# A row-tiled pair for the half-filled rows of unseparated projections, the output weights in two transfers, and a new timetable, in a transformer block

## The chip, the core and the metric

The kernel runs on one core of a Trainium2 chip. The metric is the time of one execution on the device in microseconds; the median of the runs is compared. TensorE (PE, with its weight loads shown as PEld) multiplies, VectorE (DVE), ScalarE (ACT) and GpSimd (POOL) work on elements, and SyncE (SP) issues nearly all DMA transfers.

## The reference

One transformer block in bf16 on 2048 tokens of width 576: layer norm, attention with 32 heads of 18 and a running memory over 4 segments of 512 tokens, residual, layer norm, a feed-forward of width 4608, residual.

```python
h = x + _A_ref(_layernorm(x), wq, wk, wv, wo, beta)
h2 = h + _B_ref(_layernorm(h), w1, b1, w2, b2)
# _A_ref, for each segment s of 4, per head:
p = _softmax(qs @ ks.T * scale + causal_mask)
a_dot = p @ vs
pq = phi(qs)                       # phi(t) = t + 1 where t > 0, else exp(t)
a_mem = (pq @ M) / (pq @ z + 1e-06)
o = g * a_mem + (1.0 - g) * a_dot  # g = sigmoid(beta)
M, z = M + phi(ks).T @ vs, z + phi(ks).sum(over tokens)
# after all segments: o @ wo; _B_ref: gelu(x @ w1 + b1) @ w2 + b2
```

## The kernel before

The work of a segment is cut into stages, and the names below are the tags of its operations. X normalises four tiles of 128 tokens and brings them into transposed form: the first ones by TensorE (`TX`), the others by a store to DRAM (`X1dma`) and a transposing load (`X1flip`). P projects each tile to q, k and v and writes q and k out padded (`qkst`); transposing loads (`A0flip`, `A1flip`, ...) bring them back for the attention. A computes scores (`st`), exponentials (`exp`), causal masks (`mask`), weighted values (`val`) and, from segment 1 on, the read of the memory (`mem`); M adds to the memory. B is the output projection, the residual (`hadd`), the second layer norm and its transposition, C the first feed-forward product with its evictions (`copy`) and the gelu, D the second product and the last residual. Stages of different segments overlap.

The width of 576 is four blocks of 128 rows and one of 64. The weights hold a fifth block, k = 4, in which the first 288 output columns have their last 64 rows in partitions 0 to 63, the other 288 in partitions 64 to 127; the remaining partitions of that block are zero. A projection of one tile (`proj_pair`) has two forms:

- Separated. `fn_a` (P) runs, for each of five blocks, two matmuls with 64 rows each, side by side on the two row halves of TensorE, the upper half for one half of the columns (one PSUM bank), the lower for the other. Then a marker on DVE or POOL (`pass`) separates the halves, and `fn_b` (R) runs four more such pairs with the banks exchanged. That is 10 + 8 matmuls, in nine pairs. Other work stands between P and R.
- Unseparated (`fused`), when the timetable puts R right behind P: ten full matmuls of 128 rows, five for each half of the columns, the zero partitions included.

TensorE thus works in four modes: full, two row tiles of 64, four row tiles of 32 (scores), and four column tiles of 32 (values, and some reads of the memory).

The order of the work is written out by hand as data. `TIMETABLE` gives for each operation a rank and an engine; `Graph.schedule` sorts by rank, runs a cost model in which each operation has planned costs, and picks buffers and PSUM banks. The costs in the `add` calls are planned costs in microseconds: they decide which buffer is taken, not what is issued. Each engine then executes its instructions in that order, and waits in the order's place when something isn't ready. SyncE too issues its transfers in the order of the timetable, `load_w` with one transfer for a whole weight. In the modes' part of `schedule`, a change of mode is planned with 0.1 us.

Of the kernel before, what the change touches and what calls it, by code (L numbers as in the profile page):

```python
# [11 lines left out]
ACT = mybir.ActivationFunctionType  # L12
# [7 lines left out]
FUSED = 1.225  # L20
INF = 1e9
# [322 lines left out]
}  # L344


# [1278 lines left out]
```

## Time and profile before

| | |
|---|---|
| median of 3 runs | 440.25 us (439.9 to 440.84) |
| span of the profiled execution | 439.3 us; the page gives no time of that execution beside it |
| TensorE busy | 431.0 us (98%), 5182 matmuls, granted clock 1.000 |
| DVE, ACT, POOL busy | 288.5, 298.2, 176.5 us |
| DMA | 75.61 MB, 172 GB/s |

In a row of groups stand line, engine, operation, what it writes and reads, shapes and count, then busy time, mean ns of one, and the idle time of the engine before it with what ended it. Matmuls are pipelined, so the duration of one is longer than the time in which the next follows. The chain of waits lists start, length and what in order of time; two matmuls side by side on row tiles count as two.

### The profile page before, as it was taken

What the parts mean: (1) busy time and instruction counts of PE and PEld (TensorE: products, weight loads), DVE (VectorE), ACT (ScalarE), POOL (GpSimd) and SP (SyncE); (2) the same over time, 40 slices, a digit from 0 to 9 for tenths busy, and PEclk for the clock granted to TensorE, in tenths of its full rate; (3) what the DMA queues carried; (4) which work ended last, traced back from release to release, by engine and by line L of the source; (5) the groups of instructions that cost most, each with busy time, mean ns of one, the idle gap of its engine ahead of it and who ended that gap; (6) DMA issues with size and microseconds to landing.
All of it is one profiled execution on the core that took longest, in us unless ns stands there. A gap on an engine that the chain in (4) does not pass through costs nothing.

```text
span 439.3 us, 12412 instructions
## 1 busy us (share of the span) xinstructions
PE 431.0 (98%) x5182; PEld 279.0 (64%) x5182; DVE 288.5 (66%) x641; ACT 298.2 (68%) x325; POOL 176.5 (40%) x328
## 2 busy tenths in 40 slices
PE   8998999999999999999999999999999999999997
PEld 5665677776677676664445766654457785446886
DVE  5898889988997987975698897766776211000002
ACT  5997988999888897788898976657864003465000
POOL 6676866445867644571631462320203001020001
PEclk9999999999999999999999999999999999999999
DMA  7699999989899758973671859506405752450011
GB/s 229 214 209 230 347 262 273 234 274 229 236 235 340 196 157 231 229 157 101 155 185 26 243 152 213 107 18 213 140 25 143 233 131 81 151 175 1 1 58 51
DMA packets 80280, 75.61 MB, mean 172 GB/s; under 512 B 57952, under 2 KB 67424, under 8 KB 80224
## 3 DMA queue, kind: packets, MB, share of 16 engines
q1 hardware_dynamic: 80080, 74.74, 63.9%
q8 instruction: 40, 0.66, 0.7%
q14 instruction: 16, 0.13, 0.1%
q10 hardware_dynamic: 144, 0.09, 0.1%
HBM read 42.30 MB, written 18.87 MB: 139 GB/s over the span
## 4 chain that ended last, share of the span: by engine, by line
PE 89%; DMA 4%; DVE 3%; SPq 1%; POOL 1%; ACT 1%; issue 1%; DVEq 0%; POOLq 0%
PE bank L1453 33%; PE bank L1364 24%; PE bank L859 9%; PE bank L1401 8%; PE bank L1227 4%; PE bank L885 3%; PE bank L1252 3%; DMA xreg<-xnd 2%; DMA x<-in_A_x_dram 2%; PE bank L1201 1%; PE bank L1098 1%; PE bank L1067 1%; SPq L663 1%; SPq L670 1%; PE bank L1198 1%
## 5 line engine op out<-in xcount | busy, mean ns | idle before, releaser
L1016 ACT ACTIVATE pt<-bank 128x1024 bf16<-128x1024 f32 x160 | 155.5, 1021 | 36.7 <-PE bank L1227 26.5
L1453 PEld LDWEIGHTS <-hT 128*128 128x128 bf16 x1188 | 111.3, 98 | 33.4 <-issue 6.6
L1364 PE MATMUL bank<-xreg,w1g 64*128 64x512 bf16 x972 | 107.7, 377 | 0.0
L1364 PEld LDWEIGHTS <-w1g 64*128 64x128 bf16 x972 | 46.2, 94 | 57.2 <-issue 3.0
L1453 PE MATMUL bank<-w,hT 128*128 128x288 bf16 (+2 forms) x594 | 77.8, 283 | 0.0
L1453 PE MATMUL bank<-w_lo,hT 128*128 128x288 bf16 (+2 forms) x594 | 77.6, 283 | 0.0
L1466 DVE TENSOR_TENSOR ot<-bank,hc 128x288 bf16<-128x288 f32 (+2 forms) x33 | 14.1, 444 | 85.1 <-PE bank L1453 79.6
L1241 POOL TENSOR_SCALAR_AFFINE_SELECT pt<-pt 128x512 bf16<-128x512 bf16 x57 | 38.0, 680 | 45.4 <-ACT pt L1016 45.1
L1369 ACT ACTIVATE hT<-bank,b_col 128x512 bf16<-128x512 f32 x36 | 22.1, 690 | 46.4 <-PE bank L1364 46.3
L1439 POOL TENSOR_TENSOR hc<-hc,b_bc 128x576 f32<-128x576 f32 x11 | 14.5, 1333 | 83.6 <-DMA hc<-hd 83.6
L1379 DVE TENSOR_SCALAR hT<-bank,b_col 128x512 bf16<-128x512 f32 x45 | 32.6, 742 | 19.4 <-PE bank L1364 17.3
L1401 PE MATMUL bank<-xreg,w1g 64*128 64x256 bf16 x648 | 38.4, 270 | 0.0
L1401 PEld LDWEIGHTS <-w1g 64*128 64x128 bf16 x648 | 30.5, 94 | 6.6 <-issue 3.2
L1384 ACT ACTIVATE hT<-hT 128x8192 bf16<-128x8192 bf16 (+2 forms) x6 | 31.8, 5320 | 0.1
L859 PE MATMUL bank<-hT,xreg 64*128 64x288 bf16 x414 | 27.7, 283 | 1.7 <-DMA xreg<-xnd 1.7
L885 PE MATMUL bank<-hT,xreg 128*128 128x288 bf16 x210 | 28.4, 287 | 0.3 <-ACT pt L1016 0.2
L1412 DVE TENSOR_TENSOR hT<-bank,b_col 128x512 bf16<-128x512 f32 x33 | 21.4, 681 | 6.3 <-PE bank L1401 5.9
L1377 ACT ACTIVATE hT<-bank,b_col 128x512 bf16<-128x512 f32 x27 | 17.8, 686 | 11.4 <-PE bank L1364 11.0
L859 PEld LDWEIGHTS <-xreg 64*128 64x128 bf16 x414 | 19.6, 94 | 8.3 <-DMA xreg<-xnd 1.9
L1227 PE MATMUL bank<-qk 32*128 32x512 bf16 (+3 forms) x384 | 24.2, 301 | 0.2 <-DVE hT L1379 0.2
L885 PEld LDWEIGHTS <-xreg 128*128 128x128 bf16 x210 | 19.7, 98 | 6.4 <-issue 1.0
L773 POOL TENSOR_TENSOR ln<-ln,mhalf 128x1 f32<-128x1 f32 x32 | 19.5, 610 | 2.7
(122 smaller groups left out, 566.4 us busy)
## 6 DMA issues: line engine op xcount, KB each, us to landing
w1g<-in_B_w_dram SPq DMA_DIRECT2D x41, 576.0 KB, 4.9
qkd<-qk_pad SPq DMA_DIRECT2D x15, 512.0 KB, 4.7
hd<-h SPq DMA_DIRECT2D x16, 288.0 KB, 4.6
hc<-hd SPq DMA_DIRECT2D x16, 288.0 KB, 4.0
w_lo<-in_B_w_dram SPq DMA_DIRECT2D x3, 864.0 KB, 7.2
w<-in_B_w_dram SPq DMA_DIRECT2D x3, 864.0 KB, 8.4
xb<-in_A_x_dram SPq DMA_DIRECT2D x16, 144.0 KB, 4.7
x2d<-xn SPq DMA_DIRECT2D x14, 160.0 KB, 2.8
```

Source lines behind the costliest of these rows:

```text
L859: return nc.tensor.matmul(out=half(hf), lhsT=xTb.t[r, k, ts], rhs=wt[r, hf, k, :], start=start, stop=stop, skip_group_check=True)
L885: nc.tensor.matmul(out=half(hf), lhsT=xTb.t[:, k, ts], rhs=wt[:, hf, k, :], start=(k == 0), stop=(k == KT - 1))
L1016: ops.append(add(prio, {"act": 1.04}, lambda e, j=j: nc.scalar.activation(out=pt.t[:, 2 * j:2 * j + 2, :], in_=st[j].t[:], func=ACT.Exp, s ...
L1227: nc.tensor.matmul(out=st[i // 2].t[:, i % 2, off:off + n_], lhsT=qk[rows, 1, kt * P:(kt + 1) * P], rhs=qk[rows, 0, kt * P:L], start=True, ...
L1241: nc.gpsimd.affine_select(out=blk, in_=blk, pattern=[[0, 4], [1, P]], compare_op=ALU.is_ge, fill=0.0, base=0, channel_multiplier=-1)
L1364: nc.tensor.matmul(out=cc[w].t[:], lhsT=w1.t[rows, k, q, :], rhs=x2T[s].t[rows, k, :], start=(k == 0), stop=(k == ND - 1))
L1369: ready_f[f + w] = [add(pf - 12, {"act": 0.68}, lambda e, f=f, w=w, cc=cc: nc.scalar.activation(out=hT[:, :, f + w, :], in_=cc[w].t[:].rea ...
L1379: nc.vector.tensor_scalar(out=dst, in0=src, scalar1=b, scalar2=None, op0=ALU.add)
L1384: ge = add(2.9, {"act": 0.42 * (f1 - f0) + 0.2}, lambda e, f0=f0, f1=f1: nc.scalar.activation(out=hT[:, :, f0:f1, :], in_=hT[:, :, f0:f1, ...
L1401: nc.tensor.matmul(out=cc[w].t[:, q * 2 * P:(q + 1) * 2 * P], lhsT=w1.t[rows, k, q, :], rhs=x2T[s].t[rows, k, ts], start=(k == 0), stop=(k ...
L1412: nc.vector.tensor_tensor(out=dst, in0=src, in1=b.unsqueeze(2).to_broadcast([P, 2, 2 * P]), op=ALU.add)
L1453: nc.tensor.matmul(out=c.t[:, 0:c1 - c0], lhsT=hT[:, tl // 2, f, (tl % 2) * P:(tl % 2 + 1) * P], rhs=w2_c[ch][:, f - ch * WCH, c0:c1], sta ...
```

## The change

An unseparated projection may now take a third form: the four full blocks as full matmuls, and the fifth block as one pair of matmuls with 64 rows, on the two row halves side by side. The pair stands first (`form == "first"`) or last (`"last"`). `schedule` takes it where its cost model finds it cheaper, which is where the neighbour on the pair's side is row-tiled by 64 already. It has eight full matmuls and a pair in place of ten full ones.

The weights of the output projection are loaded in two transfers of one half of the columns each, which may be issued from the time when the first tile is transposed, in place of one transfer behind the last projection of segment 0. Some planned costs change (the first normalisations, one exponential, the gates, and the size of the broadcast of beta). All ranks of the timetable are new, and some operations change engines.

```diff
+TAILED = 1.103
...
 TIMETABLE = {
...
-    "B01tail": "g 330",
+    "B01tail": "d 326",
...
-    "C00dma": "s 261 292 319 395 399 420 421 461 466",
+    "C00dma": "s 242 315 373 374 388 415 424 438 484",
...
-    "P01copy": "a 105 114 109 92 94 143",
+    "P01copy": "d104 d117 a133 a74 a86 a143",
...
-    "X1flip": "s 198",
+    "X1flip": "s 220",
...
-    "X2dma": "s 136 258 310 266 444 400",
+    "X2dma": "s 149 347 285 190 408 401",
...
+    "wodma": "s 100 218",
...
+        for n, op in enumerate(on_pe):
+            op.next_mode = next((o.mode for o in on_pe[n + 1:] if o.mode), "full")
...
             if op.fused:
                 c = 0.0 if op.mate is not None else FUSED
-            kind = op.mode if e == "pe" else op.table
+                if op.mate is None:
+                    was, then = table.get("pe"), op.next_mode
+                    s = SWITCH["pe"]
+                    plain = FUSED + s * (was != "full") + s * (then != "full")
+                    first = TAILED + s + s * (was != "rows64") + s * (then != "full")
+                    last = TAILED + s + s * (was != "full") + s * (then != "rows64")
+                    if min(first, last) < plain - 1e-9:
+                        op.form = "first" if first <= last else "last"
+                        c = TAILED + s + s * (was != ("rows64" if op.form == "first" else "full"))
+                        table["pe"] = kind = "full" if op.form == "first" else "rows64"
...
-                return add(prio, {"dve": 0.55}, apply, [sa, sb, *after, *extra], None, [dst_buf, ma, mb, xsrc], name="apart")
+                return add(prio, {"dve": 0.70}, apply, [sa, sb, *after, *extra], None, [dst_buf, ma, mb, xsrc], name="apart")
...
+                n = KT if b.form is None else KT - 1
+                if b.form == "first":
+                    for w in range(2):
+                        rows(w, w, KT - 1, True, False)
                 for hf in range(2):
-                    for k in range(KT):
-                        nc.tensor.matmul(out=half(hf), lhsT=xTb.t[:, k, ts], rhs=wt[:, hf, k, :], start=(k == 0), stop=(k == KT - 1))
+                    for k in range(n):
+                        nc.tensor.matmul(out=half(hf), lhsT=xTb.t[:, k, ts], rhs=wt[:, hf, k, :], start=(k == 0 and b.form != "first"),
+                                         stop=(k == n - 1 and b.form != "last"), skip_group_check=True)
+                if b.form == "last":
+                    for w in range(2):
+                        rows(w, w, KT - 1, False, True)
...
-        bl = load(2, lambda: beta_bc[:], lambda: A_beta.partition_broadcast(P), 8e3, [xn_ok[0, 0]])
+        bl = load(2, lambda: beta_bc[:], lambda: A_beta.partition_broadcast(P), 250e3, [xn_ok[0, 0]])
...
-        w_ok["o"] = load_w(4, "o", 3, begin)
+        gr.tag = "wo"
+        w_ok["o"] = [load(4, lambda h=h: wts["o"][:, h, :, :].rearrange("p k d -> p (k d)"),
+                          lambda h=h: A_w[3 * P:4 * P, h * KT * HALF:(h + 1) * KT * HALF], 350e3, [xn_ok[0, 0]]) for h in range(2)]
+        gr.tag = ""
```

More of the change, by code (lines that the diff above doesn't have):

```diff
@@ L396, in __init__ @@
         self.alt, self.mate, self.fused, self.fence, self.mode = None, None, False, None, table
+        self.form, self.next_mode = None, None
 OVER = {"act": 0.1, "dve": 0.08, "pool": 0.035}
@@ L461, in schedule @@
             c = op.cost[e]
+            kind = op.mode if e == "pe" else op.table
             if op.fused:
                 c = 0.0 if op.mate is not None else FUSED
-            kind = op.mode if e == "pe" else op.table
+                if op.mate is None:
[8 more added lines that the diff above has]
+                        table["pe"] = kind = "full" if op.form == "first" else "rows64"
             if kind is not None and kind != table.get(e):
@@ L826, in stage_X @@
                 pl = prio + 0.1 * tl if s == 0 else X_PRIO + 0.3 * s + 0.05 * tl
-                ap = layernorm(pl, lambda xb=xb, tl=tl: xb.t[:, tl % 2, :], [ld] + ([xs_pre[0][1], x0b] if s == 0 else []), xb, xn, 0.50, [], tl if (s, tl) in CENTRED else None,
+                ap = layernorm(pl, lambda xb=xb, tl=tl: xb.t[:, tl % 2, :], [ld] + ([xs_pre[0][1], x0b] if s == 0 else []), xb, xn, 0.56, [], tl if (s, tl) in CENTRED else None,
                                ([ld], [ld] if tl else [x0b]) if s == 0 else None, (s, tl // 2) in PE_X)
@@ L1186, in stage_A @@
                 pg = prio + 0.001 * (5 * (g // 2) + 3 * (g % 2))
-                a = add(pg + 0.02, {"act": 0.62}, lambda e, g=g, eb=eb: nc.scalar.activation(out=eb.t[:], in_=qks[g].t[:, 0, :], func=ACT.Exp),
+                a = add(pg + 0.02, {"act": 0.64}, lambda e, g=g, eb=eb: nc.scalar.activation(out=eb.t[:], in_=qks[g].t[:, 0, :], func=ACT.Exp),
                         [qk_ok[g]], eb, [qks[g]], table="exp", name="eg")
@@ L1520, in gmz_fn @@
             nc.gpsimd.tensor_copy(out=gmz[32 * i:32 * i + 32, :, 0:Dh], in_=src.to_broadcast([32, G, Dh]))
-        gates.append(add(2.5, {"dve": 1.7}, gate_fn, [ge], name="gates"))
+        gates.append(add(2.5, {"dve": 0.73}, gate_fn, [ge], name="gates"))
         later.append(gates[0])
         mz_gates = [add(3.55, {"pool": 0.31}, lambda e, i=i: gmz_fn(i), [gates[0]], name="gmz") for i in range(4)]
-        w_ok["o"] = load_w(4, "o", 3, begin)
+        gr.tag = "wo"
+        w_ok["o"] = [load(4, lambda h=h: wts["o"][:, h, :, :].rearrange("p k d -> p (k d)"),
+                          lambda h=h: A_w[3 * P:4 * P, h * KT * HALF:(h + 1) * KT * HALF], 350e3, [xn_ok[0, 0]]) for h in range(2)]
+        gr.tag = ""
         b1_in = Buf(ot_s)
```

625 rows, old and new, of the table TIMETABLE are left out of this document.

## Prediction

> **What bounds the kernel now.** I read the page's head and its slices first, then the busy time by stretches, the chain that ended last, and the list of waits.
>
> ```profile
> span 439.3 us, 12412 instructions
> ...
> PE 431.0 (98%) x5182; PEld 279.0 (64%) x5182; DVE 288.5 (66%) x641; ACT 298.2 (68%) x325; POOL 176.5 (40%) x328
> ...
> PE   8998999999999999999999999999999999999997
> ...
> DVE  5898889988997987975698897766776211000002
> ACT  5997988999888897788898976657864003465000
> ...
> PEclk9999999999999999999999999999999999999999
> DMA  7699999989899758973671859506405752450011
> ```
>
> TensorE is busy for 98% of the span at full clock. DVE, ACT and the DMA queue are near full too, but only in the first half; from slice 5 on they change the time only if they stop TensorE. The busy time by stretches (PE, PEld, DVE, ACT, POOL; clock; DMA share; GB/s) says where TensorE does stop:
>
> ```profile
> 0.00:20.00 20.00, 18.01 (x150) 12.10 (x151) 14.31 (x40) 14.88 (x28) 12.49 (x37) 1.00 0.71 233
> 20.00:40.00 20.00, 16.97 (x324) 12.08 (x322) 19.02 (x48) 18.54 (x23) 15.29 (x33) 1.00 1.00 181
> 40.00:60.00 20.00, 19.65 (x348) 14.09 (x350) 16.88 (x42) 16.72 (x22) 14.89 (x40) 1.00 1.05 322
> 60.00:436.60 376.60, 376.39 (x4367) 240.76 (x4361) 238.04 (x512) 248.03 (x255) 133.86 (x220) 1.00 0.61 161
> ```
>
> After 60 us it idles for 0.2 of 376.6 us; from 20 to 60 us for 3.4, while DVE works 19.0 of 20 us and the DMA share is 1.00. So a change can save time in two ways: fewer columns and mode changes on TensorE, anywhere, or less idle time between 20 and 60 us. The chain shows the longest idle piece, and the list of waits prices it:
>
> ```profile
> 3.85 0.43 SPq L663
> ...
> 26.32 0.91 SPq L663
> 27.33 1.27 SPq L670
> 28.64 1.51 SPq L670
> 30.20 0.59 SPq L663
> 30.90 9.12 DMA xreg<-xnd
> 40.07 2.99 PE bank L859 x46
> ```
> ```profile
> PE bank L859 <- DMA xreg<-xnd: 1.7, 1, 1.7
> ```
>
> SyncE stores two normalised tiles of segment 1 (26.32 is the second store; 3.85 is a plain load, for comparison), issues two transposing loads for the first attention stage, then the whole output weight (30.20), then the transposing load of segment 1's second half (30.90). That one lands at 40.02, and TensorE, which had run dry 1.7 us before, starts on it at 40.07. Everything that TensorE does before 40.07 is thus worth nothing by itself: only an earlier landing is.
>
> **The change on TensorE.** Counted in the two programs: 36 separated and 24 unseparated projections become 34 and 26, and 23 of these 26 take the new form. In slots of 288 columns, where a row-tiled pair is one slot, a separated projection has 9, an unseparated one 10, the new form 9: 564 become 543, 21 fewer. Changes of tiling mode between neighbouring instructions rise from 193 to 215, because the timetable alternates more often; 22 more. Both prices stand in the chain around 166 us:
>
> ```profile
> 164.47 2.21 PE bank L1453 x18
> 166.68 1.20 PE bank L1252 x32
> 167.88 0.33 PE bank L1227 x8
> 168.21 2.31 PE bank L1453 x18
> ```
>
> The first 18 full matmuls follow a full one, the last 18 follow a row-tiled one: 2.21/18 = 0.123 us is a slot, and 2.31 - 2.21 = 0.10 us a mode change. So 21 x 0.123 = 2.58 us go and 22 x 0.10 = 2.2 us come: 0.4 us net (with 0.09 to 0.11 a change: 0.6 to 0.2). The pair inside the new form costs no change of its own where its neighbour on that side is already row-tiled by 64, and the form is taken only there. In the order of the after program some 0.3 us of the 0.4 are earned ahead of the waiting projection, where the landing swallows them; **0.1 us** counts.
>
> The Trainium skill speaks against such alternation: TensorEngine Tiling (Array Packing), section Tiling Modes, says that changing the tiling mode, and not just the tile, drains TensorE. The trace agrees that each change costs something, 0.10 us.
>
> **The change at the head.** Before 40 us the order on every engine stays almost as it was; four moves matter.
>
> ```profile
> 22.78 0.81 DVE L681 TENSOR_SCALAR v_aug<-bank,ln 128x576 bf16<-128x576 f32 x1
> ...
> 25.09 0.46 DVE L1079 TENSOR_TENSOR pt<-pt,tri 128x512 bf16<-128x512 bf16 x1
> 25.47 0.43 DVE L788 TENSOR_SCALAR xn<-x,ln 128x640 bf16<-128x640 bf16 x1
> ...
> 26.16 0.75 DVE L962 SCALAR_TENSOR_TENSOR fk_pad<-ek,rk 128x576 bf16<-128x576 bf16 x1
> ...
> 28.97 0.74 DVE L683 CAST qk_pad<-bank 128x576 bf16<-128x576 f32 x1
> ```
> ```profile
> L757 DVE BATCH_NORM_STATS2 ln<-x 128x6 f32<-128x288 bf16 x20 | 7.9, 438 | 1.2 <-DMA x<-in_A_x_dram 0.9 <-issue 0.2
> ```
>
> First, DVE gets more to do ahead of the normalisation at 25.47, whose result the stores and the flip wait for: two copies of q and k (2 x 0.74, from ACT), two masks (2 x 0.46, from POOL) and one key feature step (0.75, moved forward), less one copy of v (0.81, to ACT) and one mask (0.46): 3.15 - 1.27 = 1.9 us later. Second, the broadcast of beta is issued behind the last x tile of segment 0 instead of ahead of it:
>
> ```profile
> x<-in_A_x_dram SPq DMA_DIRECT2D x1, 160.0 KB, 6.1
> beta_bc<-in_A_beta_dram SPq DMA_DIRECT2D x1, 8.0 KB, 6.2
> ```
>
> DVE's wait for that tile, 0.9 us in the statistics' row above, can go. That leaves the normalisation 1.0 us later (0 to 1.9). SyncE makes good about half of it: the second store held it for 0.91 us at 26.32, against 0.43 for the plain issue at 3.85, and the first tile's store now goes out while DVE still works on the second. The flip is issued about 0.5 us later (0 to 1.9).
>
> Third and fourth, what lies ahead of the flip in the DMA queue (us from issue to landing):
>
> ```profile
> wt_o<-in_A_w_dram SPq DMA_DIRECT2D x1, 720.0 KB, 6.4
> w_lo<-qkd SPq DMA_TRANSPOSE x1, 3.7
> xreg<-xnd SPq DMA_TRANSPOSE x1, 9.1
> ```
>
> The transposing load issued at 28.64 landed at 32.3, the weight (30.20 + 6.4) at 36.6: 4.2 us of the queue for 720 KB. The change sends one half of it around 15 us, in the stretch with a DMA share of 0.71, and leaves the other half ahead of the flip: 2.1 us less. But a load of 320 KB of x for segment 2, which stood behind the flip, now stands ahead of the two transposing loads. At the weight's rate it takes 1.9 us; the queue is shorter where it enters (3.7 us to landing, not 9.1), so part may fit into gaps: 0.3 to 1.9, and I take 1.1, the middle. The flip then lands 0.5 - 2.1 + 1.1 = **-0.5 us**, at about 39.5 (37.9 to 41.7). One more DMA issue on SyncE, 0.4 us, is inside the half that SyncE makes good.
>
> **The rest.** Of the other idle time between 20 and 60 us (3.4 - 1.7) one piece has its cause removed: a transposition waits for a tail that POOL wrote, and DVE now writes it behind its own normalisation.
>
> ```profile
> 52.92 0.45 PE L802 MATMUL bank<-ident,xn 128*128 128x128 bf16 x5 [0.24 <-POOL xn L1309]
> ```
>
> I count **-0.3 us** for this and small waits like it (-1.4 to +0.5). The corrected costs of single steps change no instruction, only the planner's figures. Behind 60 us the evictions shift from DVE to ACT (38 instead of 30 of the feed-forward copies on ACT) and orders change in all stages; I take nothing for it: DVE and ACT have over 128 us to spare there, and TensorE idled 0.2 us. If that cover were gone, each late eviction would show as idle time of up to its 0.69 us in the last stretch.
>
> ```profile
> L1377 ACT ACTIVATE hT<-bank,b_col 128x512 bf16<-128x512 f32 x27 | 17.8, 686 | 11.4 <-PE bank L1364 11.0
> ```
>
> Sum: -0.5 - 0.1 - 0.3 = -0.9 us. Against the profiled span that is 438.4. The page gives the span alone; the runs' median, 440.25, lies 0.95 above it, and with that the forecast is 439.35, given as **439.3 us**. Some 0.2%, 0.9 us, is what a measurement of this kernel can tell from no change.
>
> **The rivals.**
> *DVE holds the flip (slower).* DVE worked 19.0 of 20 us ahead of the flip. If the 1.9 us reach SyncE whole and the x load costs its whole 1.9, the landing moves by 1.9 - 2.1 + 1.9 = +1.7 us; with the 0.1 the time is 440.25 + 1.6 = 441.85. It decides from the point where the flip is issued over 1.0 us later than at 30.90 (2.1 - 1.1). For it: a full DVE and DMA share 1.00. Against it: DVE's own wait for x and SyncE's held store. Chance 0.27.
> *The landing stays where it was (no change).* The half weight and the x load cancel and TensorE's gain is swallowed by the wait: -0.1, 440.15. For it: the DMA share of 1.00. Chance 0.24.
> *The whole wait goes (faster).* The x load fits into gaps, DVE is not late, and the 1.7 us go with the 0.4 on TensorE and 0.3 besides: -2.4, 437.85. Against it: the full queue. Chance 0.04.
> *The drain is dearer.* A matmul of 288 columns is shown with 283 ns in the row below, 160 ns beyond its slot. If each of the 22 changes cost that, 3.5 - 2.6 = +0.9: 441.15. It decides from 0.117 us a change (2.58/22), and the chain shows 0.10. Chance 0.02. This is what the rule of the Trainium skill on draining (TensorEngine Tiling (Array Packing), Tiling Modes) would come to if nothing overlapped a drain; the trace speaks against that.
>
> ```profile
> L859 PE MATMUL bank<-hT,xreg 64*128 64x288 bf16 x414 | 27.7, 283 | 1.7 <-DMA xreg<-xnd 1.7
> ```
>
> **How the numbers follow.** The forecast has 0.43; its own range, with the flip landing between 38.6 and 39.8, is 438.4 to 439.7 us, and 0.03 of it falls within 0.2%. Faster: 0.40 + 0.04 = 0.44. Within 0.2%: 0.24 + 0.03 = 0.27. Slower: 0.27 + 0.02 = 0.29. The range of 8 in 10 has to hold both signs: from 437.8, where the whole wait goes, to 441.9, where DVE holds the flip; what is left out is a stage behind 60 us that comes apart.
>
> **What would show it.** Right: the flip of segment 1 lands at 39 to 39.8 and the wait of the projection for it falls to about 1 us; busy TensorE in the last stretch begins about 0.5 us earlier; mode changes stay at 0.10 us; idle time behind 60 us stays under 0.5. Wrong: the flip is issued over 1 us later than at 30.90 and the wait stays or grows; the first residual additions wait for their x tiles, which now queue behind a 576 KB weight; or TensorE's idle time appears behind 60 us in front of a stage whose DVE work came late.

## The result, and the profile after

The changed kernel is slower: 442.15 us in the median (441.32 to 443.28) against 440.26, a ratio of 1.0046 (95% interval 1.0028 to 1.0065). Run again later it came to 441.36 against 440.25, 1.0028 (1.0007 to 1.0048). By the ratios the loss is 2.0 and 1.2 us; the forecast was a gain of 0.9, in a range that ended at 441.9 us.

The head of the page after, and the busy time by stretches (same columns as before):

```profile
span 439.6 us, 12360 instructions
...
PE 431.2 (98%) x5169; PEld 276.7 (63%) x5169; DVE 282.4 (64%) x627; ACT 302.7 (69%) x335; POOL 176.8 (40%) x332
```
```profile
0.00:20.00 20.00, 18.44 (x168) 11.81 (x169) 15.22 (x43) 15.43 (x27) 14.24 (x39) 1.00 0.81 258
20.00:40.00 20.00, 18.32 (x364) 13.20 (x362) 19.10 (x50) 18.66 (x25) 14.11 (x29) 1.00 1.10 236
40.00:60.00 20.00, 19.39 (x321) 13.42 (x316) 17.50 (x45) 17.80 (x24) 15.83 (x38) 1.00 1.03 283
60.00:436.60 376.60, 374.86 (x4325) 238.18 (x4324) 230.32 (x491) 250.81 (x263) 132.66 (x228) 1.00 0.59 159
```

From 20 to 40 us TensorE works 18.32 us where it worked 16.97: the head was won. Behind 60 us it idles 1.74 us where it idled 0.21. The chain of waits after, and the list of waits from 60 to 85 us, show where:

```profile
30.52 1.99 SPq L686
...
35.63 6.09 DMA xb<-in_A_x_dram
...
49.70 0.85 POOL xn L1333
50.60 0.51 PE bank L818 x6
...
73.24 5.17 DMA qk<-qkd
78.45 0.40 PE bank L1251 x4
...
185.11 2.31 PE bank L1477 x18
```
```profile
PE bank L1251 <- DMA qk<-qkd: 1.3, 1, 1.3
PE bank L1225 <- DVE MZacc L1022: 0.3, 1, 0.3
```

The flip of segment 1 (issued at 30.52) is no longer followed by a wait. Later TensorE waits at 50.60 for a tail that POOL wrote, at 76.7 for DVE's sum of the memory, which has to leave its bank, and at 78.45 for a transposing load of the scores' keys and queries (A1flip#0). A row-tiled change still costs 0.10: 18 full matmuls behind one take 2.31 us, as before.

To account for it all I compared the starts of neighbouring matmuls, in each trace, with the spacing of like neighbours that wait for nothing (0.0555 us at 128 columns, 0.109 at 256, 0.1225 at 288, 0.1625 at 384, 0.2155 at 512, and 0.094 for a change of mode). What is over is lost time, in us (the first matmul starts at 0.83, which the last row contains; a wait counts 0.1 to 0.2 us more here than in the list of waits, 1.42 for 1.3 at 78.45):

| stretch | before | before again | after | after again |
|---|---|---|---|---|
| 0 to 45 us | 8.89 | 8.18 | 7.05 | 7.63 |
| 45 to 60 | 0.89 | 0.95 | 1.23 | 1.28 |
| 60 to 85 | 0.47 | 0.81 | 2.24 | 0.87 |
| 85 to 145 | 1.09 | 1.11 | 1.97 | 1.95 |
| 145 to 245 | 1.31 | 1.04 | 0.89 | 0.89 |
| 245 to end | 0.73 | 0.73 | 0.73 | 1.43 |
| stream without loss | 422.19 | 422.19 | 421.69 | 421.69 |
| last matmul starts | 436.41 | 435.84 | 436.62 | 436.57 |

The stream is 0.5 us shorter, the head loses 0.6 to 1.8 us less, and 45 to 145 us give back 1.2 to 3.0. One execution isn't another, though: the two columns of one program differ by up to 1.4 us in a stretch. In the last row the two programs lie 0.5 us apart in the mean, and not 1.2 to 2.0 as by the runs, since the traced executions of before were, on average, slower than its median (about 441.0 and 440.47 us) and those of after faster (441.32 and 441.27). So the table says where time went, not how much of the runs' loss each stretch is. The experiments were therefore timed over several rounds, and each ratio below is to the kernel before on the same chip at the same time.

### The profile page after: what moved, and what is told of

Read it like the earlier page. It is cut to its first block, busy times and chain, and to the rows that moved or that the text cites. A ratio compares the mean times of both kernels' runs of the same rounds, so it can differ in the third digit from the quotient of the medians.

```text
span 439.6 us, 12360 instructions
## 1 busy us (share of the span) xinstructions
PE 431.2 (98%) x5169; PEld 276.7 (63%) x5169; DVE 282.4 (64%) x627; ACT 302.7 (69%) x335; POOL 176.8 (40%) x332
## 4 chain that ended last, share of the span: by engine, by line
PE 84%; DVE 5%; SPq 4%; DMA 3%; POOL 2%; issue 2%; DVEq 0%; POOLq 0%
PE bank L1477 33%; PE bank L1388 24%; PE bank L1425 8%; PE bank L875 6%; PE bank L1251 4%; PE bank L1276 3%; PE bank L905 3%; SPq L686 3%; DMA xb<-in_A_x_dram 1%; DVE ln L773 1%; DMA qk<-qkd 1%; PE bank L1225 1%; PE bank L1222 1%; DVE fk_pad L986 1%; DVE xn L804 1%
## 5 line engine op out<-in xcount | busy, mean ns | idle before, releaser
L1490 DVE TENSOR_TENSOR ot<-bank,hc 128x288 bf16<-128x288 f32 (+2 forms) x33 | 14.4, 443 | 87.0 <-PE bank L1477 81.0
L1265 POOL TENSOR_SCALAR_AFFINE_SELECT pt<-pt 128x512 bf16<-128x512 bf16 x58 | 41.4, 725 | 46.2 <-ACT pt L1040 46.1
L1393 ACT ACTIVATE hT<-bank,b_col 128x512 bf16<-128x512 f32 x36 | 22.4, 688 | 45.2 <-PE bank L1388 44.8
L1463 POOL TENSOR_TENSOR hc<-hc,b_bc 128x576 f32<-128x576 f32 x7 | 8.9, 1277 | 79.5 <-DMA hc<-hd 79.4
L1403 DVE TENSOR_SCALAR hT<-bank,b_col 128x512 bf16<-128x512 f32 x39 | 28.0, 743 | 15.4 <-PE bank L1388 14.9
L875 PE MATMUL bank<-hT,xreg 64*128 64x288 bf16 x436 | 32.7, 284 | 0.8 <-ACT pt L1040 0.8
L1401 ACT ACTIVATE hT<-bank,b_col 128x512 bf16<-128x512 f32 x33 | 21.3, 685 | 10.8 <-PE bank L1388 10.6
L875 PEld LDWEIGHTS <-xreg 64*128 64x128 bf16 x436 | 20.9, 94 | 11.0 <-issue 5.4
L905 PE MATMUL bank<-hT,xreg 128*128 128x288 bf16 x180 | 25.0, 287 | 0.0
L1436 DVE TENSOR_TENSOR hT<-bank,b_col 128x512 bf16<-128x512 f32 x31 | 20.4, 676 | 4.4 <-PE bank L1425 4.3
L1263 DVE TENSOR_TENSOR pt<-pt,tri 128x512 bf16<-128x512 bf16 x38 | 18.8, 511 | 5.8 <-ACT pt L1040 5.6
```

Source lines behind the costliest of these rows:

```text
L875: return nc.tensor.matmul(out=half(hf), lhsT=xTb.t[r, k, ts], rhs=wt[r, hf, k, :], start=start, stop=stop, skip_group_check=True)
L905: nc.tensor.matmul(out=half(hf), lhsT=xTb.t[:, k, ts], rhs=wt[:, hf, k, :], start=(k == 0 and b.form != "first"), stop=(k == n - 1 and b.f ...
L1265: nc.gpsimd.affine_select(out=blk, in_=blk, pattern=[[0, 4], [1, P]], compare_op=ALU.is_ge, fill=0.0, base=0, channel_multiplier=-1)
L1393: ready_f[f + w] = [add(pf - 12, {"act": 0.68}, lambda e, f=f, w=w, cc=cc: nc.scalar.activation(out=hT[:, :, f + w, :], in_=cc[w].t[:].rea ...
L1401: nc.scalar.activation(out=dst, in_=src, func=ACT.Identity, bias=b)
L1403: nc.vector.tensor_scalar(out=dst, in0=src, scalar1=b, scalar2=None, op0=ALU.add)
```

## The experiments

**What the profiled execution stood for.** The kernel before, unchanged (e1).

> The kernel before, unchanged. The after program is 1.9 us slower by the medians, but its profiled span (439.6) is only 0.3 us above the one of before (439.3). Theory A (the loss is in the program, and the two profiled executions were not typical): the time agrees with before within 0.4 us, and its span scatters by about 0.5 us or more around 438.7, so that the span of 439.3 was one of the longer ones of before. Rival B (the loss lies outside the span, in what comes ahead of the first and behind the last instruction): spans of before lie at 439.3 again and the time is about 0.95 us above the span, against 1.7 us in after.

Measured 440.46, ratio 0.9999 (0.9981 to 1.0018); its runs reach from 438.45 to 442.46 and their spans from 436.7 to 440.7. Time less span is 1.7 to 1.8 us in every run, of before as of after (440.47 - 438.8 in the profiled one, 441.32 - 439.6 in after's). So the execution of before that the prediction read took about 441.0 us, 0.7 over the median: theory A. Its wait for the flip is one of the things that vary. The issues of before again, and of the kernel before with the new form (e7), which issues the same weight ahead of the flip:

```profile
xreg<-xnd SPq DMA_TRANSPOSE x1, 8.8
```
```profile
xreg<-xnd SPq DMA_TRANSPOSE x1, 7.9
```

Issued at 30.46 and 30.48, they landed at 39.27 and 38.37; TensorE lost 1.5 us in the one and nothing in the other, 1.7 in the trace of the prediction (40.02). So TensorE needs it at about 37.8 to 38.4 us.

**The weights in two transfers, alone** (e4, and once more as e16): the two loads of the change in place of the one, in the timetable of before.

```diff
-    "dma": "s 1 12 13 39 28 195 144 262",
+    "dma": "s 1 12 13 39 28 144 262",
+    "wodma": "s 97.5 195",
```

> The kernel before with one part of the change alone: the output weights in two transfers of half the columns, the first issued behind the first x load of segment 1 (about 15 to 20 us), the second in the old place ahead of the transposing load X1flip. Order, forms and all other ranks are those of before. Theory A (the flip lands late because of the 720 KB ahead of it): it lands 2 us or more earlier than 40.02, the wait of 1.7 us on TensorE goes, and the time falls by 1.4 to 1.7 us against before, to about 438.7. Rival B (the stages behind 60 us give such a gain back even in the order of before, because they wait for something with a date of its own): the wait at 40 us goes, other waits grow between 50 and 130 us, and the time falls by less than 0.5 us.

> The kernel before with the output weights in two transfers, run once more. It was 0.87 us faster than before by the medians in one call (interval -1.6 to -0.3), and its neighbour with the second half behind the load 0.14 us faster in another (-0.7 to +0.8). Theory A (the wait of 0 to 1.7 us at 39 us is gone in every execution): -0.6 to -0.9 us. Rival B (the wait is rare in before, and the first figure was luck): within 0.3 us of before.

439.51, ratio 0.9978 (0.9964 to 0.9993), and again 439.69, 0.9984 (0.9966 to 1.0003). The flip landed at 38.34 and 36.61, and the wait was gone in both traces. That is 0.7 to 0.9 us, half of what the one profile promised. Before doesn't always wait, but of the four traces with the whole weight ahead of the flip (before, e1, e7, e15) three wait 1.5 to 1.7 us, so this may not be the whole reason. This version beats after clearly, and before by the two results taken together (the second interval alone just reaches 1).

**The weight behind the flip instead** (e11: the whole one, rank 195 to 198.5; e12: of e4, the second half).

> The kernel before with one transfer moved by one place: the whole output weight (720 KB) is issued behind the transposing load X1flip instead of ahead of it. Theory A (the load waits for the weight's bytes): it lands at 35 to 36.5, ahead of the 38.4 at which TensorE needs it, the weight at about 40, before its first use; the time falls as with the weights in two transfers, by 0.8 to 0.9 us against before, 439.5. Rival B (bytes behind it in the queue hold a transposing load up as well as bytes ahead of it): it lands at 38 to 40 as before, and the time stays within 0.3 us of before.

> The kernel before with the output weights in two transfers, the first behind the first x load of segment 1, the second behind X1flip instead of ahead of it. Theory A: the load lands at 35 to 36.5, and since TensorE needs it at about 38.4 nothing is won over the version with one half ahead of it (landing 37.3 and 38.3): 439.5, -0.8 against before. Rival B (the one half ahead still makes the load late in some executions): 439.1, -1.2, with a narrower spread.

440.13, ratio 1.0002 (0.9983 to 1.0021), and 439.9, 1.0002 (0.9985 to 1.0019). With the whole weight behind it the flip landed at 35.54, as theory A said, yet the time stayed. The next load behind the weight, the first x tile of the residual, paid for it; the chain of waits of e11, and DVE's timeline:

```profile
37.23 6.56 DMA xb<-in_A_x_dram
```
```profile
43.89 1.55 DVE L1304 TENSOR_TENSOR h<-bank,xb 128x288 f32<-128x288 f32 x4 [1.64 <-DMA xb<-in_A_x_dram]
```

TensorE, which needs a bank that this addition frees, lost 0.9 us at 44.4 to 44.8. For the second version I can name no such wait; its trace is as good as those of the split, and the difference to e4 and e16 may be chance.

**The head of after undone** (e6: both halves ahead of the flip, `"wodma": "s 217 218"`).

> The kernel after with both halves of the output weights issued directly ahead of the transposing load X1flip, as before the change; all else as after. The half weight of 360 KB is thus back ahead of the flip. Theory A (what TensorE gains at 40 us is taken back anyway by waits for work of other engines between 50 and 85 us): the flip lands 2 us or more later than 35.36 and a wait of 0.5 to 2 us appears at 39 us, but the waits at 50.6, 76.7 and 78.5 us shrink by about as much, and the time stays within 0.4 us of after. Rival B (the gain at the head is worth its full size): the time rises by 1.5 to 2 us.

442.04, ratio 1.0043 (1.002 to 1.0065). The flip landed at 37.65, 1.7 to 2.3 us later than in the two traces of after, still before it was needed: no wait appeared. Neither theory: the expected wait did not come, and 0.7 us against after again is within the scatter.

**The new form.** Taken out of after (`b.form = None` ahead of the matmuls, e3); put into before by the form's part of the diff alone (e7); and both that and the split weights in before (e8).

> The kernel after with the order and the weights in two transfers kept, but with ten full matmuls in every unseparated projection: the new form is not used. Counted in the two programs: 23 more slots at 0.123 us (+2.8 us) and 18 fewer changes of tiling mode (197 instead of 215) at 0.093 to 0.10 us (-1.7 to -1.8). Theory A (the stream on TensorE costs what was counted): +1.0 us against after, about 443.1. Rival B (a mode change is dearer than counted, and the new form is what makes after slow): from 0.16 us a change on, the time doesn't rise; at 0.25 us it falls by 1.7, to 440.5.

> The kernel before with the new form alone, in its own order: 19 of 24 unseparated projections take it. Counted: 19 fewer slots at 0.123 us (-2.34 us), and 17 more changes of mode (193 to 210) at 0.093 to 0.10 us (+1.6 to +1.7), because a pair beside a neighbour in another mode than the row-tiled one by 64 brings a change of its own. Theory A (the prices hold, and part of it lies ahead of waits): -0.4 to -0.7 us against before, 439.7 to 440.0. Rival B (a change is dearer in the middle of a projection than between stages): from 0.138 us a change on nothing is left, at 0.2 us +1.1.

> The kernel before with the new form and with the output weights in two transfers, the first behind the first x load of segment 1; its order is otherwise that of before. Weights alone gave -0.9 us. Theory A (the two add, since one takes a wait and the other shortens the stream behind it): -1.3 to -1.6 us against before, about 438.9. Rival B (the stream runs into dates of other engines between 50 and 130 us, as in after): no better than the weights alone, -0.9 us, 439.5.

After without it: 441.34, ratio 1.0022 (1.0005 to 1.0038), no slower than with it. Its stream is 1.1 us longer, as counted, but 45 to 145 us lose 3.6 us, in place of 5.4 and 4.1. Before with it: 440.41, 0.9998 (0.9979 to 1.0017); before with it and the split: 440.17, 0.999 (0.9966 to 1.0014), no better than the split alone. So the form is worth nothing that can be measured. In the order of after its columns run into waits; in that of before the counted 0.6 to 0.7 us lie inside the interval.

**Single waits of after taken away.** The two transposing loads exchanged (e2); a feed-forward group moved ahead of the waits at 76.7 and 78.5 us (e9); both, and a product of the memory moved (e10). Beside them after unchanged (e5).

```diff
-    "A1flip": "s 482 395 474 566 589 659 727 782",
+    "A1flip": "s 474 395 482 566 589 659 727 782",
-    "C00F1": "p 368 358 402 444 425 495 452 488 502",
+    "C00F1": "p 368 358 402 444 425 495 452 478 502",
-    "M2M": "p 692 721",
+    "M2M": "p 711 721",
```

> The kernel after, with the ranks of two transposing loads of segment 1 exchanged (A1flip#0 and A1flip#2), so that the one needed first is issued first and takes the place that comes free first. In the after trace the scores of segment 1 wait 1.42 us at 78.45 for A1flip#0. Theory A (this wait and what follows from it gives the head's 2.7 us back): the wait goes, the time falls by 1.0 to 1.4 us against after, to about 440.9 (+0.6 against before). Rival B (another wait takes its place, or the cause of the median lies elsewhere): the time stays within 0.4 us of after, 441.8 to 442.5.

> The kernel after, with one group of the feed-forward product (C00F1#7, 36 row-tiled matmuls, 2.14 us), which stands ready behind the waits of 76.7 and 78.5 us, moved ahead of both. Theory A (waits at a fixed place of the order are where after loses): the 0.45 us that the read of the memory waits for a bank go, and so do the up to 1.42 us for the transposing load; by the share of traces that show the second one (3 of 5, 0.7 us in the mean) the time falls by about 1.1 us against after, to about 440.5. Rival B (the stream only runs earlier into the next waits, at 105 to 127 us and 271 us): less than 0.4 us, 441.2 to 441.6, with those waits longer by what is gained.

> The kernel after with three moves together: the feed-forward group ahead of the waits at 76.7 and 78.5 us, the two transposing loads of segment 1 in the order of their use, and the first product of the memory of segment 2 (M2M#0) behind a projection that is ready, since it waits 0.28 us at 113.7. Theory A (these waits are the loss): -1.1 to -1.5 us against after, 440.0 to 440.5, level with before. Rival B (a lead on TensorE is taken back by the next late step, whatever it is): under 0.5 us, 441.1 to 441.6.

> The kernel after, unchanged, for its spread beside that of before (438.5 to 442.7 us in 47 runs) and for a second trace. Theory A (fixed waits: the list of waits between 50 and 130 us is the loss): 442.0 us, a spread as wide as that of before, and the same waits again, at 50.6, 76.7, 78.5 and 105 to 127 us, 3.5 us together. Rival B (the loss is in the run-to-run part, landings of DMAs that differ between executions): a wider spread than before, and in the second trace other waits than in the first.

441.73 (1.0033, 1.0015 to 1.0051), 441.32 (1.0038, 1.0019 to 1.0057) and 441.82 (1.0041, 1.0022 to 1.006): none is faster than after by more than chance. In the trace of e2 the wait for the load is gone and that for DVE stays; in e9 and e10 waits that weren't there before stand at 79 to 87 us. My theory A fell here: it seems that not the place in the order, but something behind the waits sets the date. The second trace of after (e5) has the same wait for DVE, and the wait for the load, 1.4 us in the first, is absent, the load having landed at 76.88 instead of 78.41:

```profile
PE bank L1225 <- DVE MZacc L1022: 0.3, 1, 0.3
```

**DVE.** Busy time from 60 to 80 us, of before again and of after:

```profile
60.00:80.00 20.00, 19.60 (x370) 14.83 (x364) 18.49 (x40) 17.77 (x16) 12.54 (x28) 1.00 1.13 270
```
```profile
60.00:80.00 20.00, 18.39 (x353) 13.67 (x353) 19.66 (x41) 17.26 (x16) 12.84 (x28) 1.00 1.03 242
```

DVE works 19.66 of 20 us in after; over the whole span it is at 64%. Nearly the same operations take it longer. The groups from 40 to 80 us (busy, mean ns), of before again, then of after:

```profile
L788 DVE TENSOR_SCALAR xn<-x,ln 128x640 bf16<-128x640 bf16 x6 | 2.6, 431 | 0.0
L1191 DVE SCALAR_TENSOR_TENSOR e<-e,r 128x512 bf16<-128x512 bf16 x1 | 0.7, 693 | 0.3 <-issue 0.3
```
```profile
L804 DVE TENSOR_SCALAR xn<-x,ln 128x640 bf16<-128x640 bf16 x6 | 3.3, 552 | 0.0
L1215 DVE SCALAR_TENSOR_TENSOR e<-e,r 128x512 bf16<-128x512 bf16 x1 | 1.1, 1122 | 0.0
```

The timeline of after suggests why; DVE, then GpSimd:

```profile
58.97 1.27 DVE L1436 TENSOR_TENSOR hT<-bank,b_col 128x512 bf16<-128x512 f32 x2
60.17 0.82 DVE L804 TENSOR_SCALAR xn<-x,ln 128x640 bf16<-128x640 bf16 x1
...
60.14 0.66 POOL L984 TENSOR_SCALAR rk<-qk_pad 128x576 bf16<-128x576 bf16 x1
```

The normalisation was issued 0.03 us after GpSimd's operation had begun, and ended 0.18 us behind its end (60.98 against 60.80); in before again, at 58.28, it takes 0.43. The two evictions from PSUM ahead of it lie beside GpSimd too, and take 1.27 us, against 1.29 in before again. Three such overlaps in after (normalisations of 0.80 and 0.82 at 58.24 and 60.17, and the step of 1122 ns) come to 1.2 us against the durations of before again; a mask of 0.85 at 65.88, which stood on GpSimd in before, comes on top.

Three kernels test it: the four steps moved out of the overlaps (e13), DVE work left out of after (e14: one of two passes of segment 3's statistics, 1.75 us), and the same work added to before (e15).

```diff
-    "X2apply": "d 287 241 387 380",
+    "X2apply": "d 287 241 370.7 370.5",
-    "A03mask": "g399 d419 g420 ...
+    "A03mask": "g399 g419 g420 ...
-    "A1pq": "d 541 461 ...
+    "A1pq": "d 541 457.5 ...
```
```diff
-                for c in range(2):
+                for c in range(1 if x3 else 2):         # e14, x3: segment 3
+                for c in (0, 0, 1) if x3 else range(2): # e15
```

> The kernel after, with four steps of DVE moved so that they don't run beside an operation of GpSimd: two normalisations of segment 2 (X2apply#2 and #3) ahead of the step that GpSimd waits for, one reciprocal-and-multiply step (A1pq#1) ahead of a normalisation, and one mask (A03mask#1) on GpSimd. In the after trace these four last 0.81, 0.81, 1.12 and 0.85 us, without contention 0.43, 0.43, 0.69 and 0. Theory A (DVE sets the date at 76.7 us and behind it, and the contention is why): DVE is done 1.8 us earlier at 76 us, the wait of 0.45 us at 76.7 goes and TensorE idles 0.8 to 1.2 us less between 60 and 130 us; the time falls by as much, to 440.3 to 440.8. Rival B (DMA landings or bank places set it): under 0.4 us, 441.2 or more.

> The kernel after, with half of the statistics of segment 3 left out (one of two passes over each of its four tiles, which makes the normalisation of that segment another one): 4 x 0.44 = 1.75 us less work on DVE at 53, 62, 67 and 70 us, nothing moved. Theory A (DVE sets the date): TensorE idles 0.8 to 1.2 us less between 60 and 130 us, and the time falls to 440.3 to 440.8. Rival B: it stays within 0.4 us of after, DVE having a gap where it had none.

> The kernel before, with one pass of the statistics of segment 3 done twice: 1.75 us more work on DVE at 53 to 71 us, nothing moved. DVE works 18.3 to 19.0 of 20 us there, so 1.0 to 1.7 us of it fit into gaps. Theory A (DVE near its limit): a wait of 0.3 to 0.8 us appears between 70 and 85 us, +0.3 to +0.8 us, 440.6 to 441.1. Rival B (DVE has room): within 0.2 us of before.

e15: 441.39, ratio 1.0021 (1.0002 to 1.004), 0.9 us slower; TensorE waits for an eviction by DVE at 70.3 us, as in no other trace of that order:

```profile
PE bank L1403 <- DVE hT L1414: 0.3, 1, 0.3
```

So DVE is near its limit there in before already. But e13 gave 442.17 (1.004, 1.0015 to 1.0066) and e14 441.53 (1.0033, 1.0011 to 1.0056): no gain. In e13 the two normalisations take 0.76 us together by order alone,

```profile
57.63 0.76 DVE L804 TENSOR_SCALAR xn<-x,ln 128x640 bf16<-128x640 bf16 x2
```

DVE had its gaps (18.78 and 18.96 of 20 us from 60 to 80 us), the wait for it at 76.7 was gone, and A1flip#0 stood behind it. The waits of TensorE from 60 to 85 us, of e13 and e14:

```profile
PE bank L1251 <- DMA qk<-qkd: 0.4, 1, 0.4
```
```profile
PE bank L1253 <- DMA qk<-qkd: 1.6, 1, 1.6
```

**Both at once.** e13 with the two loads in the order of their use (e17), and e14 with the same (e18).

> The kernel after with the four moved steps of e13 and the two transposing loads of segment 1 in the order of their use, as in e2. Theory A (two late items in a row, DVE and a transposing load, each of which covers the other): TensorE idles 0.5 to 0.7 us between 60 and 85 us, as in the order of before, in place of 0.9 to 2.2 us, and the time falls by 0.7 to 1.0 us against after, to +0.2 to +0.6 us against before. Rival B (the loss lies elsewhere, between 85 and 145 us and at 250 to 271 us): within 0.4 us of after, +0.8 us or more against before.

> The kernel after with half of the statistics of segment 3 left out, as in e14 (1.75 us less on DVE), and the two transposing loads in the order of their use, as in e2. Theory A: as for e17, +0.2 to +0.6 us against before, and TensorE idles less than 0.6 us between 60 and 85 us. Rival B: +0.8 us or more against before.

441.04, ratio 1.0011 (0.9996 to 1.0026), and 440.82, 1.0016 (1.0005 to 1.0026): by the ratios 0.5 and 0.7 us over before, by the medians 0.8 and 0.6, where after has 1.2 and 2.0. So e17 falls on theory A's side by the ratio and on rival B's by the median. About half of the loss seems to be gone, but that is not shown: the intervals overlap with that of after again, and after itself was not timed beside these two. From 60 to 80 us TensorE is busy for 19.89 and 20.00 us:

```profile
60.00:80.00 20.00, 19.89 (x375) 14.93 (x374) 18.63 (x39) 17.93 (x16) 14.87 (x31) 1.00 1.09 250
```
```profile
60.00:80.00 20.00, 20.00 (x383) 15.31 (x383) 19.03 (x40) 18.42 (x17) 13.14 (x30) 1.00 1.05 250
```

From 60 to 85 us e17 and e18 lose 0.70 and 0.31 us, where after loses 2.24. After again, with its load in time, loses 0.87 and is busy for 19.72 of those 20 us, so a single trace proves little here. The waits fit two late items in a row, of which each covers the other: without the load's lateness DVE's wait is left (e2, after again), without DVE's the load's (e13, e14), without both almost nothing (e18), and in e17 0.28 us for DVE.

From 85 to 145 us both still lose 2.00 and 1.73. That stretch loses 1.05 to 1.31 us in all nine traces with the order of before, 1.50 to 2.56 in all eleven with that of after, in short waits at 105, 113, 114, 122 to 127 and 143 us. No experiment moved these, but the traces place two of them beside overlaps of DVE and GpSimd too. At 105 us TensorE waits 0.20 us for a marker on GpSimd that takes 0.39 us beside a normalisation, where most markers take 0.10; this is so in all eleven. At 114 us it waits 0.27 us for DVE, whose two steps ahead of it take 1.21 and 1.27 us beside GpSimd; this is so in ten of the eleven. In the other one, e3, the first of these steps takes 0.69 us, and TensorE doesn't wait there. The lines of after, then of e3:

```profile
104.84 0.58 DVE L804 TENSOR_SCALAR xn<-h,ln 128x576 bf16<-128x576 f32 x1
105.06 0.39 POOL L881 MEMSET mark_pool<- 128x1 f32 x1 [0.84 <-PE bank L875]
...
110.74 1.21 DVE L1215 SCALAR_TENSOR_TENSOR e<-e,r 128x512 bf16<-128x512 bf16 x1
...
112.53 1.27 DVE L986 SCALAR_TENSOR_TENSOR fk_pad<-ek,rk 128x576 bf16<-128x576 bf16 x1
```
```profile
110.51 0.69 DVE L1216 SCALAR_TENSOR_TENSOR e<-e,r 128x512 bf16<-128x512 bf16 x1
```

These two waits are about half of what this stretch loses more than in before; the rest stays open.

## Why the prediction was wrong

*The base.* The forecast was added to a span that is 0.5 us above another one of the same program, with a wait for the flip of 1.7 us in it, which varies (1.5 in before again, none in e7), and 0.95 us was put between span and time, where it is 1.7. The median was right as a base for the time; the wait was not one for the gain.

*The flip, the mis-sized term.* Its landing was to move by -0.5 us, to 39.5; it moved to 35.36 and 35.95. Issue: 30.52 and 31.11, about as before and not 0.5 later, so DVE's 1.9 us did not reach SyncE and the rival "DVE holds the flip" has nothing for it. Then 4.8 us from issue to landing in place of 9.1:

```profile
wt_o<-in_A_w_dram SPq DMA_DIRECT2D x1, 360.0 KB, 4.5
...
xreg<-xnd SPq DMA_TRANSPOSE x1, 4.8
```

How much of this is the half weight's depends on the order. In that of before it is the 2.1 us of the forecast in the mean (7.3 and 5.9 from issue to landing in e4 and e16, against 7.9 to 9.1). In that of after the flip took 5.9 us with the whole weight ahead again (e6), and 4.7 to 6.0 in the ten traces with one half:

```profile
xreg<-xnd SPq DMA_TRANSPOSE x1, 5.9
```

So almost 3 us of the shortening came with the rest of the new order, and what did it was not found. The 1.1 us for the x load did not show at the flip but ahead of it: the last transposing load before the weight takes 5.3 to 6.4 us in the order of after, 3.7 to 4.0 in that of before. (The forecast's lower end for the landing, 37.9, also leaves out the 0.3 us that the x load was to cost at least; with it the terms give 38.2.) Of the earlier landing only what TensorE would have waited is worth anything: 0.7 to 0.9 us in the time by e4 and e16.

*The stream: right in sum, wrong in one reason.* The stream is 0.5 us shorter (0.4 forecast), and 0.1 was taken as the part that counts; without the form after is no slower. But 18 of the 22 additional changes come from the form itself (197 changes without it, 215 with it), not from a timetable that alternates more. "The form is taken only there" was wrong: the planner takes it between two stages in another row-tiled mode too, for 1.103 + 3 x 0.1 = 1.403 against 1.225 + 2 x 0.1 = 1.425 planned us. Each such use saves a slot of 0.123 and pays a change of 0.10.

*The small waits, -0.3.* 45 to 60 us lose 0.3 us more, not less. The wait for the one tile's tail is gone, but TensorE now loses 0.77 us at 50.6 to the other tile's, which stayed on POOL. That copy takes 0.84 us, where the one that TensorE waited for in before took 0.24; it starts 0.01 us behind a step of DVE and ends 0.1 us behind that one's end (50.54 against 50.44). DVE and POOL of after, then POOL of before:

```profile
49.69 0.75 DVE L986 SCALAR_TENSOR_TENSOR fk_pad<-ek,rk 128x576 bf16<-128x576 bf16 x1
...
49.70 0.84 POOL L1333 COPY xn<-xn 128x64 bf16<-128x64 bf16 x1
```
```profile
52.62 0.24 POOL L1309 COPY xn<-xn 128x64 bf16<-128x64 bf16 x1
```

In e3 the same copy misses that step and takes 0.34 us, and TensorE doesn't wait for it.

*"I take nothing for it": the step that failed.* What stood behind 60 us cost 0.9 us from 60 to 85 and 0.9 from 85 to 145, as means of the two traces each. The argument was that DVE and ACT have 128 us to spare there. They do, from 60 to 436 us, but by the slices of the page most of it lies behind 340 us; from 60 to 80 DVE had 1.5 in before again and 0.3 in after. The prediction named what would show this, idle time behind 60 us in front of late DVE work, but gave it no price and no chance. The Trainium skill has the rule that was missing: SBUF — State Buffer, section SBUF: two separate sides, says that DVE and GpSimd share a pair of ports as an exclusive lock; when DVE's operation runs in a two-port mode or reads two inputs from SBUF (the latter only against a GpSimd operation that reads SBUF), the one that comes second stands still until the other's whole instruction is done. The trace agrees (0.82 us for 0.43, ended 0.18 us after GpSimd; and the other way round 0.84 for 0.24). A change of order that moves work of the two engines beside each other thus makes it longer, with no instruction added. Summed over the kinds of DVE operations that overlaps lengthen, they take 14.4 to 14.8 us beyond their undisturbed time in the whole span of before and of after alike (two traces each), but from 45 to 145 us 2.6 us in before and 5.5 in after. That this is behind a good part of the 1.8 us is likely, not shown: taking overlaps away ahead of 76 us brought no time by itself (e13), and no experiment took away those behind 85 us.

*The drain.* The price of 0.10 us a change stood.

## What to carry to other kernels

Read an engine's spare time in the stretch where its work is due, not over the span; and when order changes, look at which operations of VectorE come to lie beside GpSimd's, for the durations of both change. A wait of one execution is a sample: before pricing its removal, see how it varies, and count only what the next late item leaves. If removing one wait brings nothing, try removing the next one with it before dropping the theory.

## What the runs showed of the hardware

One program's DMA landings vary by more than the changes that were studied: the same transposing load landed 7.9 to 9.1 us after its issue behind the same 720 KB (the four traces in which they stand ahead of it in one transfer: before, e1, e7 and e15), another at 76.88 or 78.41, and with each TensorE lost 1.4 to 1.7 us or nothing. The 35 runs of before in one session reach from 438.5 to 442.7 us.

A normalisation of VectorE on bf16 tiles in SBUF that starts just after an operation of GpSimd lasts until 0.18 us after that one's end, a mask until 0.28 and the step of 1122 ns until 0.54 us (in after, at 60.17, 65.88 and 73.53). Over the twenty traces, 460 of 476 of these three kinds last longer than alone when they start during an operation of GpSimd on more than one column with at least 0.25 us still to run. GpSimd is held by VectorE as well (the copy of 0.84 us). Evictions from PSUM beside GpSimd kept their time, 1.27 us for two against 1.29.
